# New positions for every task of a planned kernel (linear attention followed by a softplus layer)

## The chip, the cores and the metric

The kernel runs on one core of one Trainium2 chip. The metric is the device time of one execution in microseconds (us). TensorE is called PE, its weight loads PEld, VectorE DVE, ScalarE ACT, GpSimd POOL, and SyncE, which issues nearly all DMAs, SP.

## The reference

There are 8 batches of 8 heads, 576 tokens each, 64 wide. The second layer takes all 4608 tokens with 512 features.

```
kv  = einsum('bhsd,bhse->bhde', k, v)
out = einsum('bhsd,bhde->bhse', q, kv)
rms = sqrt(mean(out * out, axis=-1, keepdims=True) + 1e-06)
x   = (out / rms * g_norm)            # heads joined: 4608 x 512, float32
h   = x @ w_in                        # w_in 512 x 2048, float64
g   = maximum(h, 0) + log1p(exp(-abs(h)))
y   = g @ w_out                       # w_out 2048 x 512, float64; y float32
```

## The kernel before

All work is cut into some 3,000 tasks: a run of matmuls, one operation of ACT, DVE or POOL, or one DMA (or a few). Each task has an engine, a list of tasks that it follows, buffers ("slots" of numbered rings) that it takes and gives back, and a position, a number that says how urgent it is: less is earlier. A planner (`Plan.order`) runs the tasks through a model of the engines with fixed costs; whenever several tasks of an engine could start at about the same time, the one of the least position goes first. What comes out is an order for each engine, and the program is issued in it. The hardware then runs each engine's list strictly in that order and waits by semaphores. So positions change no instruction, only the order of each engine's list, and with it which buffer of a ring a task gets.

The stages overlap and are these:

- Attention, for each batch: k and v are loaded (`kv_of`, L706 and L704) and multiplied by five groups of products on PE (L717), the last of them for the tail of 64 tokens; ACT copies the result (L725). For each tile of 128 tokens (`rows`), q is loaded (L787; L620 for batches 2 to 7) and turned (on PE, L797, with a copy L804, or on DVE, L772), the row products (L741) follow, ACT squares (L814), DVE sums (L745), POOL takes the root (L748, L749), DVE multiplies (L753), and the result is turned again (L759 on PE with a copy, or L841 on DVE) and stored as x.
- Weights: w_in and w_out come as float64 words in 16 chunks of 128 (L434). ACT and DVE make float32 of them (`weight`: ACT L445 and L462, DVE L449, L453, L458, L466, L471, and L479 or L477), and split each into three rounded parts for fast products (`split_weight`, ACT L517 and L533, DVE L520 and L525). Chunks from the fifth on are also stored and loaded again later (`w_spill`).
- Plain steps: the first two blocks of 384 tokens are multiplied with chunks 0 to 3 in plain float32 (`plain_step`: first layer L934, softplus L954, second layer L940). Block 0 does its first two steps tile by tile.
- Chunk steps: the other ten blocks are multiplied with chunks 0 to 3 (blocks 2 and 3) or 0 to 5 in three rounded products each (`step`: L889 with twelve products, softplus L911, split L913, L900 and L904, second layer L896 with nine).
- Wide steps: for the other chunks, nine blocks of 512 tokens and two chunks at a time, by seven products instead of eight (`wide_step`, `units_of`). In each of 48 steps PE makes seven groups of six products (L1127, units 0 to 6) into one pair of banks. ACT copies partial results between banks (L1169 after units 0 and 1, L1173 after unit 3; unit 4 adds to what L1173 reads and copies), softplus follows (L1155), and the split (ACT L1185, DVE L1188 and L1191), then eight groups of three second-layer products (L1198). The steps form two phases; a block's sums are stored at the end of a phase and added at the start of the next (L970), and results leave by L991.
- While PE has nothing else to do at the start, the planner fills in warm-up products (L1292).

Where positions come from: constants of the lists P0 to P8 are added to a step number. P0 gives conversions and loads of the first weights (`CONVERT`, `FETCH`) and offsets of attention (`EARLY`), P1 the loads and splits of the wide stage's weight pairs 2 to 7 (`SPLIT`, first the load, then the split), P2 the loads and conversions of chunks 6 to 15 (`TAKEN`), P3 offsets within wide steps (`MM2`, `LATE`, `SPLIT_G`), P4 the tiles, P5 the batches, P6 the units of each wide block, P7 the loads of the first two batches, P8 the splits of the first four chunks (`DIVIDE`). One task sets the manner for all:

```python
small = [o for o in options if engine == "PE" and o[1].kind != "all"]
...
at, t = min(options, key=lambda o: (o[1].pos, o[0]))
```

and the wait that ties a DMA to a point of PE's progress, besides its buffer:

```python
for t in plan.tasks:
    if t.behind is not None and t.behind >= 0:
        t.after.append([m for at, m in mm1s if at <= t.behind][-1])
```

Of the kernel before, what the change touches and what calls it, by code (L numbers as in the profile page):

```python
# [60 lines left out]
class Plan:  # L61
# [19 lines left out]
    def slot(self, ring):  # L81
        return Slot(ring)

    def add(self, engine, ns, run, after=(), pos=0.0, take=(), give=(), size=0, behind=None, follows=None, kind="all"):
        pos, behind = round(pos, 4), None if behind is None else round(behind, 4)
        t = Task(engine, ns, run, [a for a in after if a is not None], pos, list(take), list(give), size)
        for s in t.give:
            s.readers += 1
        self.tasks.append(t)
        t.follows = follows  # L90
        t.behind = behind
        t.kind = kind
        return t
# [113 lines left out]
def kernel(  # L207
# [44 lines left out]
    STEPS = [(ph, n, p) for ph in (1, 2) for n in range(n_wide) for p in PAIRS[ph - 1][n]]  # L252
    LAST = 2

    P0 = [-31.3, -30.64, -54.26, -2.58, -36.38, -151.12, -27.16, 4.44, -244.63, -199.65, -214.44, -165.6, -164.44, -156.26, -159.89, -75.56, -23.5, -59.34, 26.17, 9.55, 6.93, 9.91, -11.55, 6.49, 1.74, 171.93, 45.23, 8.24, -1.35, 6.07]
    P4 = [-65.4, -44.7, 24.9, -3.29, -25.77, -68.08, -27.61, -41.6, -20.58, -7.41, -5.23, 2.97, 0.94, -0.53, -8.96, -41.17, 23.47, 21.42, -2.21, 21.68, 32.94, 28.75, -0.37, -0.34, 15.51, 20.06, -16.32, -5.39, 6.85, 4.85, -5.3, -4.14, 5.1, -2.49, -15.14, -6.44]
    P5 = [-6.87, 19.59, -28.05, -5.0, -6.56, -14.19, 6.28, -0.65, -1.35, 132.48, 5.39, 2.29, -35.85, 1.03, -3.98, -2.82]
    P6 = [1.5, 9.94, 2.49, -38.82, -78.8, -70.82, -46.98, -61.55, -42.52, -70.31, 9.49, -78.96, -19.23, -24.63, 6.03, 1.34, -86.15, 2.77]
    P7 = [-204.42, -204.37, -115.29, -133.71, -205.37, -112.22, -110.08, -112.78, -124.83, -118.61, -140.44, -143.0, -146.99, -143.39, -131.27, -137.05, -122.31, -132.54, -123.82, -86.56, -103.79, -107.89, -154.07, 73.6, -145.36, -62.81, -36.39, -58.6, 23.67, -42.55]
    CONVERT, FETCH, EARLY, LATER = P0[:8], P0[8:16], P0[16:27], P0[27:]  # L260
    P1 = [57.49, 48.45, 65.67, 68.82, 125.79, 131.21, 6.34, 52.11, 67.59, 160.94, 164.07, 162.57]
    P2 = [23.98, 35.63, 26.02, 37.56, 45.23, 74.16, 67.95, 125.34, 102.58, 112.94, 164.02, -30.15, 114.21, 131.81, 139.56, -30.3, 132.2, -22.69, 106.41, 131.82, -7.6]
    P3 = [1.03, 0.05, 7.95, -2.68, 0.96, 2.95, 4.31, -8.29, 3.44, 4.08, 0.91, 1.99, -0.13, -36.22, 0.66, -1.76]
    SPLIT = {p: (P1[i], P1[6 + i]) for i, p in enumerate((2, 3, 4, 5, 6, 7))}
    TAKEN = {c: (P2[c - 6], P2[4 + c]) for c in range(6, 16)}
    LEAD, APART, AHEAD, MM2, LATE, SPLIT_G = P3[0], P3[1], P3[2], P3[3:11], P3[11:14], P3[14]
    EARLIER = P3[15]
    P8 = [-29.7, 133.87, -29.82, -14.38, -36.33, 52.16, -9.84, -27.11]
    DIVIDE, BANKED, STORE, AFTER = P8, False, 1.0, 1.5
    BY_TILES, CHAIN = 2, False  # L270
    PACE = 2.5
# [338 lines left out]
    def load_q(b):  # L610


        q_slots[b], q_loads[b] = slot("qa"), []
        pos = x_pos(first_tile[b] + 1) - EARLY[7] + P5[B + b]

# [67 lines left out]
    def x_pos(t):  # L683

        n = t // TB
        return P4[t] + t * EARLY[0] + EARLY[1] if n == 0 else P4[t] + first_step["block", n] - (EARLY[2] if n == 1 else EARLY[3]) + t % TB * (len(CHUNKS[n]) // TB)

    def kv_of(b):

        pos = x_pos(first_tile[b]) - (EARLY[4] if b else EARLY[5]) + P5[b]
        bank = slot(f"s{b}" if b < 2 else "tp")
        last = first = None
        MAIN = 4 * P
        for p in range(NP + 1):
# [4 lines left out]
            def load(src, s, p=p, tail=tail, n=n, ks=ks):  # L701
                if tail:
                    s.tile = tails[s is not ks]
                    nc.sync.dma_start(out=s.tile[:n], in_=src[b, :, MAIN:].rearrange("h s d -> s h d"))  # L704
                    return
                nc.sync.dma_start(out=new(s, [P, 2, 4, D]), in_=src[b, p::NP, :MAIN].rearrange("h (s i) d -> s h i d", i=4))  # L706

            lds = [add("SP", 500, lambda src=src, s=s, load=load: load(src, s), (), pos - EARLY[6] + 0.5 * p + (P7[2 * (5 * b + p) + of_v] if b < 2 else 0), [s], [],
                       650 if tail else 850, behind=pos - 5.5) for of_v, (src, s) in enumerate(((k, ks), (v, vs)))]
# [18 lines left out]
    def rows(t):  # L728
# [38 lines left out]
        for b, r0, n, s0 in parts(t):  # L767
# [26 lines left out]
            def turn_q(n=n, q_s=q_s, at_qa=at_qa, tp=slot("tp" if t < AT_ONCE else "o")):  # L794
                y = new(tp, [P, NP, P])
                for p in range(NP):
                    nc.tensor.transpose(y[:, p, :n], pairs(natural(q_s, at_qa)[:n], p), ident[:n, :n])  # L797

            tp = turn_q.__defaults__[-1]
            ld = add("SP", 900, load, (), pos - EARLY[7] + P7[20 + t], [q_s] if not at_qa or t == 0 else [], [], 1220 * n // P,  # L800
                     behind=pos - 3.5, follows=first_load[0] if t and at_qa else None)
# [218 lines left out]
    def units_of(ph, n):  # L1020

        at = starts[first_of[ph, n]] - LEAD + P6[n_wide * (ph - 1) + n]
        held = {}
# [236 lines left out]
    for c in range(KF):  # L1260
        for j in (2 * c, 2 * c + 1):
# [3 lines left out]
            else:  # L1265
                fetch, pos = (x + P2[20] * (j % 2) for x in TAKEN[c])
                weight(j, pos, fetch, fetch)
# [60 lines left out]
```

## Time and profile before

| | |
|---|---|
| time, median of 3 runs | 863.43 us (863.42 to 865.5) |
| profiled execution | 863.93 us, its span 861.8 us, granted clock 0.999 |
| PE busy / PEld busy | 849.1 us (99%) / 742.5 us (86%) |
| DVE / ACT / POOL busy | 694.4 us (81%) / 489.5 us (57%) / 76.5 us (9%) |
| chain that ended last | PE 93%, DMA 4%, ACT 1%, DVE 1% |
| DMA | 167.06 MB, mean 194 GB/s |

The span runs from the first to the last instruction of the profiled execution; its time is 2.13 us longer. Ends of matmuls are modelled, so a short wait of PE shows as a longer distance between the starts of two products and not always as idle time. L1127 stands for line 1127 of the kernel; a line of the profile gives output and inputs by buffer names without their numbers, and `pieces`, `w`, `units`, `early` and others are pieces of memory that serve several rings.

### The profile page before, as it was taken

How to read it: one execution, taken by the hardware profiler on the slowest of the kernel's cores; microseconds unless marked ns; L12 is line 12 of the kernel's file. 1: busy time of each engine (PE TensorE's matmuls, PEld its weight loads, DVE VectorE, ACT ScalarE, POOL GpSimd, SP SyncE). 2: the span in 40 equal slices, each digit the busy share in tenths (PEclk: the TensorE clock that was granted, in tenths of full speed). 3: DMA queues.
4: the chain of work that ended last, by engine and by line, in shares of the span. 5: the costliest groups of instructions: out<-in, count | busy, mean ns of one | idle time of the engine just before them, and what ended most of it. 6: DMA issues, size and time to landing. Idle time of an engine off the chain costs nothing.

```text
span 861.8 us, 16844 instructions
## 1 busy us (share of the span) xinstructions
PE 849.1 (99%) x6405; PEld 742.5 (86%) x6405; DVE 694.4 (81%) x974; ACT 489.5 (57%) x921; POOL 76.5 (9%) x79
## 2 busy tenths in 40 slices
PE   7999999999999999999999999999999999999998
PEld 5755888999898999989988888889888989899986
DVE  4988898888788888898987788787878767778873
ACT  3656554445444556656656555555757555566654
POOL 0433142221113100000000000000000000000000
PEclk9999999999999999999999999999999999999999
DMA  9998999778882766447544545556445654677754
GB/s 260 269 246 272 250 233 277 160 241 229 220 187 80 198 189 197 135 134 233 184 143 143 179 139 192 172 158 215 144 158 167 204 167 138 216 223 242 245 179 138
DMA packets 239777, 167.06 MB, mean 194 GB/s; under 512 B 106320, under 2 KB 198736, under 8 KB 239696
## 3 DMA queue, kind: packets, MB, share of 16 engines
q1 hardware_dynamic: 239392, 165.86, 65.4%
q8 instruction: 50, 0.82, 0.4%
q14 instruction: 31, 0.25, 0.1%
q10 hardware_dynamic: 304, 0.13, 0.1%
HBM read 112.98 MB, written 52.95 MB: 193 GB/s over the span
## 4 chain that ended last, share of the span: by engine, by line
PE 93%; DMA 4%; ACT 1%; DVE 1%; SPq 1%; POOL 0%; issue 0%; ACTq 0%; DVEq 0%
PE banks L1198 30%; PE banks L1127 28%; PE banks L889 14%; PE banks L896 14%; PE banks L741 2%; PE banks L717 2%; PE banks L934 2%; PE banks L940 2%; DMA g<-in_moe_w_out_dram 1%; DMA m<-w_spill 1%; DMA raw<-in_moe_w_in_dram 1%; DMA loads<-in_v_dram 1%; DMA part<-m 1%; PE banks L759 0%; POOL roots L749 0%
## 5 line engine op out<-in xcount | busy, mean ns | idle before, releaser
L1198 PE MATMUL banks<-w,gv 128*128 128x512 f32 x408 | 126.4, 391 | 0.0
L1198 PE MATMUL banks<-pieces,gv 128*128 128x512 f32 x360 | 111.7, 391 | 0.0
L1127 PEld LDWEIGHTS banks<-units,w 128*128 128x128 f32 x744 | 97.5, 188 | 9.2 <-ACT banks L1173 5.2
L1127 PE MATMUL banks<-units,w 128*128 128x256 f32 x744 | 104.6, 284 | 0.1
L1188 DVE TENSOR_TENSOR gv<-gv,g_True 128x1024 fp32r<-128x1024 f32 x47 | 57.5, 1223 | 46.1 <-ACT gv L1185 46.1
L889 PE MATMUL banks<-units,pieces 128*128 128x384 f32 x480 | 91.3, 338 | 0.0
L889 PEld LDWEIGHTS banks<-units,pieces 128*128 128x128 f32 x480 | 84.2, 188 | 3.3 <-issue 0.5
L1127 PE MATMUL banks<-units,pieces 128*128 128x256 f32 x600 | 82.9, 282 | 0.0
L1127 PEld LDWEIGHTS banks<-units,pieces 128*128 128x128 f32 x600 | 78.6, 188 | 4.3 <-ACT banks L1173 0.7
L911 ACT ACTIVATE half<-banks 128x384 f32<-128x384 f32 x56 | 27.5, 490 | 92.9 <-PE banks L889 86.7
L1198 PE MATMUL banks<-w,g_False 128*128 128x512 f32 x204 | 79.3, 389 | 0.0
L1198 PEld LDWEIGHTS banks<-w,gv 128*128 128x128 f32 x408 | 70.5, 188 | 9.4
L1198 PE MATMUL banks<-pieces,g_False 128*128 128x512 f32 x180 | 70.1, 390 | 0.0
L1198 PEld LDWEIGHTS banks<-pieces,gv 128*128 128x128 f32 x360 | 61.5, 188 | 7.5
L896 PE MATMUL banks<-pieces,gv 128*128 128x512 f32 x270 | 67.0, 392 | 0.0
L749 POOL TENSOR_TENSOR roots<-roots,half 128x8 f32<-128x8 f32 x36 | 62.8, 1744 | 3.0
L1155 ACT ACTIVATE g_True<-banks 128x256 f32<-128x256 f32 x96 | 36.7, 384 | 45.8 <-PE banks L1127 44.9
L1090 DVE TENSOR_TENSOR units<-units,loads 128x1024 fp32r<-128x1024 f32 x42 | 51.3, 1221 | 11.3 <-ACT units L1087 10.9
L896 PE MATMUL banks<-w,gv 128*128 128x512 f32 x234 | 58.8, 393 | 0.2 <-DVE gv L904 0.2
L1191 DVE SCALAR_TENSOR_TENSOR g_False<-gv 128x1024 fp32r<-128x1024 f32 x47 | 57.5, 1223 | 1.1
L896 PEld LDWEIGHTS banks<-pieces,gv 128*128 128x128 f32 x270 | 50.0, 188 | 8.7
L1093 DVE SCALAR_TENSOR_TENSOR units<-units 128x1024 fp32r<-128x1024 f32 x42 | 51.4, 1224 | 2.3
(126 smaller groups left out, 1562.4 us busy)
## 6 DMA issues: line engine op xcount, KB each, us to landing
loads<-x SPq DMA_DIRECT2D x180, 128.0 KB, 2.6
part<-m SPq DMA_DIRECT2D x72, 256.0 KB, 3.1
m<-part SPq DMA_DIRECT2D x72, 256.0 KB, 3.8
loads<-form SPq DMA_DIRECT2D x45, 256.0 KB, 3.4
form<-loads SPq DMA_DIRECT2D x36, 256.0 KB, 2.5
raw<-in_moe_w_in_dram SPq DMA_DIRECT2D x16, 512.0 KB, 4.7
loads<-in_k_dram SPq DMA_DIRECT2D x30, 256.0 KB, 5.0
loads<-in_v_dram SPq DMA_DIRECT2D x30, 256.0 KB, 5.1
```

Of the source, the lines that this page charges most:

```text
L717: nc.tensor.matmul(kv[e * D:(e + 1) * D, i if tail else p], lhsT=l, rhs=r, start=(p == 0 and i == 0), stop=tail, skip_group_check=True)
L749: nc.gpsimd.tensor_tensor(out=r.tile, in0=r.tile, in1=half, op=ALU.pow)
L889: nc.tensor.matmul(from_the_end(hp, w), lhsT=w_in.tile[:, i, kd * P:(kd + 1) * P], rhs=from_the_end(xv.tile[:, i, kd], w), start=(m == 0), ...
L896: nc.tensor.matmul(mine[i].tile, lhsT=gv.tile[:, m, i * P:(i + 1) * P], rhs=w_out.tile[:, m], start=(c == cs[0] and m == 0), stop=(c == cs ...
L911: a = add("ACT", 490, lambda: nc.scalar.activation(new(g, [P, NT]), h.tile, func=AF.Softplus, scale=BACK), [a], s, [g], [h])
L1090: nc.vector.tensor_tensor(out=part_of(1, F32R), in0=part_of(0), in1=xl.tile if m > 1 else xl.tile[:, 0], op=ALU.subtract)
L1093: nc.vector.scalar_tensor_tensor(out=part_of(2, F32R), in0=part_of(1), scalar=RADIX, in1=part_of(0), op0=ALU.mult, op1=ALU.add)
L1127: nc.tensor.matmul(from_the_end(place(q), (16, 8)[kd]), lhsT=w[:, m, at:at + P], rhs=from_the_end(dst.tile[:, m, v, kd] if u < 6 else dst. ...
L1155: nc.scalar.activation(dst, src, func=AF.Softplus, scale=BACK)
L1188: nc.vector.tensor_tensor(out=gvt(1, F32R), in0=gvt(0), in1=gt(), op=ALU.subtract)
L1191: nc.vector.scalar_tensor_tensor(out=gt(F32R), in0=gvt(1), scalar=RADIX, in1=gvt(0), op0=ALU.mult, op1=ALU.add)
L1198: nc.tensor.matmul(from_the_end(mine[i].tile, P), lhsT=(gvt(m, F32R) if m < 2 else gt(F32R))[:, c, i * P:(i + 1) * P], rhs=from_the_end(ou ...
```

## The change

All numbers of P0, P1, P2, P3, P4, P5, P6, P7 and P8 are replaced. Nothing else is touched: the same tasks with the same dependencies, rings and model of the planner, and the first two blocks still in plain float32. The lists of all engines come out in a new order; the program has one warm-up product more (34 instead of 33) and otherwise the same instructions.

```diff
-    P0 = [-31.3, -30.64, -54.26, -2.58, -36.38, -151.12, -27.16, 4.44, -244.63, -199.65, -214.44, -165.6, -164.44, -156.26, -159.89, -75.56, -23.5, -59.34, 26.17, 9.55, 6.93, 9.91, -11.55, 6.49, 1.74, 171.93, 45.23, 8.24, -1.35, 6.07]
...
-    P7 = [-204.42, -204.37, -115.29, -133.71, -205.37, -112.22, -110.08, -112.78, -124.83, -118.61, -140.44, -143.0, -146.99, -143.39, -131.27, -137.05, -122.31, -132.54, -123.82, -86.56, -103.79, -107.89, -154.07, 73.6, -145.36, -62.81, -36.39, -58.6, 23.67, -42.55]
+    P0 = [-26.53, -8.6, -26.43, -24.39, -7.46, -30.31, -30.51, -0.46, -18.19, -11.95, -60.72, -23.11, -7.51, -6.45, -6.97, 1.51, -96.36, -87.58, 23.05, 9.66, 5.63, 70.22, -11.32, 5.48, 1.28, 13.64, -24.06, 10.03, 2.31, 2.8]
...
+    P7 = [223.82, 237.85, 234.17, 234.67, 233.72, 224.13, 258.05, 213.66, 244.82, 245.6, 18.63, 20.59, 18.78, -10.12, 26.9, 20.69, 26.52, 26.35, 25.8, 26.37, 159.02, 240.48, 142.45, 87.4, 36.17, 16.65, 55.56, 45.85, 25.93, -10.94]
     CONVERT, FETCH, EARLY, LATER = P0[:8], P0[8:16], P0[16:27], P0[27:]
-    P1 = [57.49, 48.45, 65.67, 68.82, 125.79, 131.21, 6.34, 52.11, 67.59, 160.94, 164.07, 162.57]
-    P2 = [23.98, 35.63, 26.02, 37.56, 45.23, 74.16, 67.95, 125.34, 102.58, 112.94, 164.02, -30.15, 114.21, 131.81, 139.56, -30.3, 132.2, -22.69, 106.41, 131.82, -7.6]
-    P3 = [1.03, 0.05, 7.95, -2.68, 0.96, 2.95, 4.31, -8.29, 3.44, 4.08, 0.91, 1.99, -0.13, -36.22, 0.66, -1.76]
+    P1 = [56.7, 48.36, 57.86, 71.7, 122.92, 131.34, 49.33, 64.2, 68.62, 81.9, 167.23, 29.07]
+    P2 = [26.08, 34.69, 22.87, 44.8, 34.85, 56.63, 53.72, 108.5, 124.7, 118.83, 132.01, -7.51, 132.17, 132.06, 131.34, -7.51, 127.41, 52.53, 132.4, 132.35, -6.49]
+    P3 = [0.23, 0.22, 10.44, -2.21, 0.7, 2.68, 4.22, -2.49, 2.69, 2.73, 0.68, 2.26, -0.04, -94.1, -87.17, -2.98]
     SPLIT = {p: (P1[i], P1[6 + i]) for i, p in enumerate((2, 3, 4, 5, 6, 7))}
     TAKEN = {c: (P2[c - 6], P2[4 + c]) for c in range(6, 16)}
     LEAD, APART, AHEAD, MM2, LATE, SPLIT_G = P3[0], P3[1], P3[2], P3[3:11], P3[11:14], P3[14]
     EARLIER = P3[15]
-    P8 = [-29.7, 133.87, -29.82, -14.38, -36.33, 52.16, -9.84, -27.11]
+    P8 = [-24.8, 69.82, -7.38, -23.22, -18.55, -21.72, -19.14, -30.61]
```

## The prediction

> **What bounds the kernel now.** I read the page's busy times first, then the busy times cut into stages, then TensorE's (PE's) timeline with what ended each gap, then the waits, and last the issue order of the two programs, which gives orders and no times.
>
> ```profile
> PE 849.1 (99%) x6405; PEld 742.5 (86%) x6405; DVE 694.4 (81%) x974; ACT 489.5 (57%) x921; POOL 76.5 (9%) x79
> ```
>
> ```profile
> 0.00:30.00 30.00, 23.41 (x306) 16.88 (x307) 17.76 (x33) 13.53 (x26) 4.95 (x11) 1.00 0.95 267
> 30.00:91.00 61.00, 59.72 (x615) 38.07 (x613) 53.10 (x88) 39.12 (x79) 21.62 (x20) 1.00 0.93 259
> 91.00:140.00 49.00, 48.22 (x594) 41.33 (x596) 43.27 (x75) 26.61 (x51) 15.03 (x15) 1.00 0.94 238
> 140.00:358.00 218.00, 217.88 (x1770) 197.64 (x1761) 184.27 (x315) 110.97 (x220) 34.94 (x34) 1.00 0.69 190
> 358.00:640.00 282.00, 282.00 (x1782) 253.19 (x1781) 235.83 (x288) 170.71 (x322) 0.00 (x0) 1.00 0.53 168
> 640.00:858.00 218.00, 217.83 (x1362) 195.34 (x1361) 159.67 (x177) 128.03 (x226) 0.00 (x0) 1.00 0.62 194
> ```
>
> The columns of the second table are the stretch in us, its length, busy us of PE, of PE's weight loads, of DVE, ACT and POOL, then the granted clock, the DMA share and GB/s. PE idles 6.6 us before 30 us, then 1.28, 0.78, 0.12, 0 and 0.17 us: 2.35 us in 828. DMA is over 0.9 busy until 140 us. So PE's own work bounds all that follows the start, and a new order can win only the start, these 2.35 us, and waits too short to show as idle. A sum over rows sizes the last: from 91.5 to 858 us stand 1152 products of L1198 and 504 of L896 at 0.227 us (2.04 for nine), 2016 of L1127 at 0.117 (2.10 for eighteen), 672 of L889 at 0.174 (2.09 for twelve), 729 us together; the attention products there take some 28 us (23 groups of L717 at 0.5, 25 of L741 at 0.65). That leaves about 9 us in 766 for all changes of shape and all waits; some 20 stretches of attention products at a quarter of a microsecond each are 5 of them, and 4 are waits.
>
> ```profile
> 19.49 0.69 PE L717 MATMUL banks<-m,m 128*64 128x64 f32 x16 [0.46 <-DMA m<-in_k_dram]
> 29.95 1.06 PE L934 MATMUL banks<-w,w 128*128 128x128 f32 x8
> 54.54 2.85 PE L934 MATMUL banks<-w,w 128*128 128x384 f32 x8
> 63.98 1.15 PE L717 MATMUL banks<-loads 128*64 128x64 f32 x32
> 117.68 0.69 PE L741 MATMUL banks<-early,w 64*64 64x64 f32 x32 [0.61 <-ACT half L911]
> ```
>
> ```profile
> 48.78 0.43 DVE L449 TENSOR_SCALAR m<-g 128x512 uint32<-128x512 uint32 x1 [0.83 <-DMA g<-in_moe_w_out_dram]
> 52.56 0.74 DVE L479 SCALAR_TENSOR_TENSOR w<-m,g_col,m 128x512 f32<-128x512 f32 x1
> ```
>
> These are the places where the start is decided: the last k load of batch 0 (19.49), the first plain product (29.95), the plain product of chunk 3 (54.54), which waited for a conversion (L479) queued behind that of another load (48.78), and the late k and v of batch 2 (63.98).
>
> ```profile
> 455.35 0.36 ACT L1173 COPY banks<-banks 128x256 f32<-128x256 f32 x1 [0.29 <-PE banks L1127]
> 455.76 1.50 PEld L1127 LDWEIGHTS banks<-units,w 128*128 128x128 f32 x12 [0.19 <-ACT banks L1173]
> 455.83 1.63 PE L1127 MATMUL banks<-units,w 128*128 128x256 f32 x12
> 457.30 0.63 PE L1198 MATMUL banks<-pieces,gv 128*128 128x512 f32 x2
> ```
>
> ```profile
> PEld banks L1127 <- ACT banks L1173: 5.9, 25, 0.6
> ```
>
> In the wide stage the weight loads waited 25 times for the copy L1173; here twelve products took 457.30 - 455.83 = 1.47 us instead of 1.40.
>
> **The change part by part.** No instruction is added or removed but one warm-up product (L1292, 33 to 34), which fills time that PE waits anyway: nothing. Every other cost is in the order.
>
> *Start.* In the issue order the last k load of batch 0 stays 16th in SP's queue, but 4352 KB stand up to it instead of 4224 (one v of batch 1 more, half a q tile less). At 267 GB/s the 128 KB are 0.5 us. What follows it to the first plain product (kv copy, two row products, two squares, two reduces, the pair of POOL roots at 2.0 us each, norm, transposition, copy) stands in the same order on ACT, DVE and POOL, with the weights of chunks 0 and 1 exchanged. So 29.95 becomes 30.4 (bounds 29.6 to 31, as the loads of w_in now go out third and not eighth).
>
> *To chunk 3.* Its w_in is now load 43 with 11920 KB up to it; before, load 43 with 12032 KB was the one that landed at 48.75. It lands at 48.3. The six conversions (0.42, 0.69, 0.69, 0.42, 0.75, 0.75) have one reduce (0.68) among them instead of a norm and the whole other conversion: ready at 52.8. PE has three groups fewer ahead of it (L759 0.44, L797 0.44, L741 0.47: 1.35), so PE on the old timing is due at 54.54 - 1.35 = 53.2. Whatever the start loses up to 0.4 us is absorbed here: net 0 (bounds -0.4 and +1.5, if the queue lags by two more k/v loads).
>
> *Late k and v of batch 2.* PE has five groups fewer ahead (0.44 + 0.86 + 2.58 + 0.44 + 0.47 = 4.8 us): due at 59.2. The last load was issued at 54.42 and is now 400 KB, 1.6 us, earlier: 52.9, plus the 6.3 us median to landing of that stretch (longest 7.1): 59.2 to 60.0. SP's queue behind it holds q loads of batch 2, which have slack. +0.2 (0 to 1.2).
>
> *Changes of shape.* Stretches of PE that leave the large products for kv or row products rise from 34 to 37, while direct kv-to-row changes fall from 7 to 4. Two kv groups in a row take 1.08 us, one alone 0.61: 0.14 for a visit on leaving, about 0.1 on entering. +0.3 (0 to 0.7).
>
> *91 to 140 us.* The row product that waited 0.61 us at 117.68 needs the bank of the one two tiles earlier; 4.9 us of PE work lay between them, now 6.9: gone (-0.6). The first L896 of the last chunk of block 2 comes 2.8 us of PE work after its L889 instead of 3.2, against ACT and DVE rows of 0.49 + 0.52 + 0.56 + 0.56 = 2.1 and some 0.5 of hand-overs: 0 to +0.5, I take 0.3. Net -0.3.
>
> *Wide stage, the copy L1173.* In 27 of the 48 steps of before exactly one product group (0.70 us) stands between the group whose result L1173 copies and the next group that writes there; now in 4. The place above is one of them: +0.07. The 23 others save 23 x 0.07 = 1.6 us; from below it is bounded by 0 (a copy behind a 1.06 us L1185 would wait all the same), from above by 23 x 0.11 = 2.5 (one LDWEIGHTS of L1127 late by more than a slot). I take -1.6. By the Trainium skill ("TensorE: Matmul & The Clock Gate", under "Architectural detail") PE pulls weight loads ahead of running products, and by that alone the wait would cost nothing and the sum would be 1.6 us higher; the trace disagrees, with 0.19 us of wait on the load and 1.47 for 1.40 on the products.
>
> *Wide stage, new tight places.* From the last group of a step to its first second-layer product before never had less than 4.8 us of PE work (bar the last step); now one step late in phase 2 has 4.2. The chain is 0.39 + 1.06 + 1.22 + 1.22 and 0.3 of hand-overs, 4.2, or 4.8 with a 0.63 softplus ahead: +0.3 (0 to 0.6). The split of the weights of pair 7 moves ahead of all other DVE and ACT work around 640 us (its position falls from 162.57 to 29.07), where DVE is 82% busy (81.97 of the 100 us from 600): +0.3 (0 to 1).
>
> Sum: 0 + 0.2 + 0.3 - 0.3 - 1.6 + 0.6 = -0.8. The span of 861.8 becomes 861.0; the profiled execution lies 2.13 us above its span (863.93), and 0.5 above the median 863.43, so the median comes to 862.6. 0.3% is 2.6 us, about what a measurement of this kernel can tell from no change.
>
> **The rivals.** *Slower: chunk 3's weight.* If the conversion of its w_in takes the 10 us that it took before (43.3 to 53.3) because its ACT half or the landing slips, it is ready at 58.3, 5.1 us after PE is due: 862.6 + 5.1 = 867.7. It decides past 8 us of conversion. For it: DMA at 0.93 and DVE at 87% of that stretch leave no reserve. Against: the order shows one foreign operation in it. 0.17.
>
> *Faster by more.* The other waits shrink too: half of the 2.35 us of idle and half of the 4 us of short waits, 3.2 us: 859.4. For it: the distances grew in most steps. Against: the tight places above. 0.22. The Trainium skill ("Perfetto Trace Analysis", Identifying the Most-Contended Engine) judges headroom by the share of LDWEIGHTS, not of matmuls; at 86% that would be up to 119 us to win. The rows speak against it: a product of 512 columns takes 0.227 us and its load 0.188, so the loader idles in a full pipe, and I give it no more than 0.02 of the 0.22.
>
> *The copy's wait only moves.* If L1173 now mostly queues behind ACT's longer rows (L1185 and L1087 at 1.06 us, L991 at 0.6), the 1.6 us stay: 864.2. For it: the order puts such a row ahead of it in many steps. Against: two groups of cover, 1.4 us, hold the copy's 0.36 and one of those rows but the longest. 0.2, still within 0.3%.
>
> **How the numbers follow.** The forecast has 0.41, the moved wait 0.2, the slower rival 0.17, the faster one 0.22. Faster by over 0.3% (under 860.8) takes the faster rival and a little of the forecast's low end: 0.24. Slower (over 866.0) takes the slower rival and a little of the unknown of the DMA order: 0.18. Within: 0.58. The range of 859.0 to 867.2 leaves out less than 2 in 10; the forecast's own is 860.8 to 864.6.
>
> **What would show it.** After: the first L934 near 30.4; the L934 x8 of chunk 3 near 53 with DVE L479 done just before; L717 of batch 2 with a short DMA wait near 59; L1173 gone from the top of the weight loader's waits (under 10 times), and no idle over 0.2 us on PE after 140. A w_in or w_out wait of several us on PE, DVE or ACT between 40 and 60 us, or DMA waits of L889 later, would make the forecast wrong.

## The result, and the profile after

The changed kernel takes 862.26 us (median of 22 runs, 860.01 to 863.9) against 863.6 us (22 runs, 861.94 to 866.08): 0.9982 of the time before, 95% interval 0.9974 to 0.9991. That is 1.3 to 1.6 us less, inside the 0.3% that was called no change, and 0.3 us from the forecast. The sum came out, by luck: its terms did not. Its profiled execution took 863.76 us with a span of 861.9.

The busy times of the page, then the same stages as before (length, busy us of PE, weight loads, DVE, ACT, POOL, then granted clock, DMA share, GB/s):

```profile
PE 848.6 (98%) x6406; PEld 746.0 (87%) x6406; DVE 695.5 (81%) x974; ACT 487.0 (57%) x921; POOL 78.6 (9%) x79
```

```profile
0.00:30.00 30.00, 23.20 (x261) 18.21 (x265) 16.06 (x30) 12.15 (x23) 4.94 (x11) 0.85 0.91 244
30.00:91.00 61.00, 59.20 (x660) 38.28 (x653) 53.25 (x89) 38.11 (x77) 24.98 (x20) 0.99 0.95 259
91.00:140.00 49.00, 48.87 (x543) 41.24 (x542) 42.85 (x72) 27.49 (x54) 9.57 (x10) 1.00 0.92 231
```

Nothing of the start is better: the clock is 0.85 in the first 30 us, where it was 1.00 (both views read 1.00 ahead of the trace's first entry for the clock, though the warm-ups stand 0.43 us apart there, and 0.23 from about 7 us on in the changed kernel, from about 11 before), and 30 to 91 us has 1.80 us of idle PE instead of 1.28. From 91 to 140 us the idle time fell from 0.78 to 0.13, as forecast. PE's timeline at the places where the start is decided:

```profile
11.47 1.97 PE L717 MATMUL banks<-loads 128*64 128x64 f32 x32 [2.85 <-DMA loads<-in_v_dram]
26.70 1.15 PE L717 MATMUL banks<-loads 128*64 128x64 f32 x32 [1.83 <-DMA loads<-in_v_dram]
32.65 1.95 PE L934 MATMUL banks<-w,w 128*128 128x128 f32 x16
55.50 2.84 PE L934 MATMUL banks<-w,w 128*128 128x384 f32 x8
62.36 1.15 PE L717 MATMUL banks<-loads 128*64 128x64 f32 x32
```

The first plain product starts at 32.65, not 30.4, chunk 3's at 55.50, not 53, and k and v of batch 2 (62.36) wait for no load. The L797 behind 26.70 takes 1.11 us where it took 0.66, at half clock. Late in the wide stage there is a wait that the forecast ruled out (no idle time over 0.2 us on PE after 140 us), lines of ACT, DVE and PE:

```profile
772.34 1.06 ACT L1087 ACTIVATE units<-loads 128x1024 fp32r<-128x1024 f32 x1 [2.40 <-DMA loads<-form]
774.58 0.68 DVE L1177 TENSOR_TENSOR g_True<-banks,g_True 128x512 f32<-128x512 f32 x1
775.32 0.98 PE L1127 MATMUL banks<-turned,half 128*128 128x256 f32 x6 [0.79 <-DVE g_True L1177]
```

A form loaded late holds ACT, DVE's L1090 queues behind ACT, and the L1177 that unit 6 needs queues behind that. What won the time shows as an absence. The row of the weight loader's waits that the prediction showed (5.9 us, 25 times) is now:

```profile
PEld banks L1127 <- ACT banks L1173: 0.4, 2, 0.2
```

To see where the time went, I took from each trace the distance from the start of one group of products to the start of the next, and subtracted what the same group takes undisturbed (L1127 0.70, a second-layer group L1198 0.68, and so on; changes of shape at their usual price). What is left is lost time, also where PE never shows as idle. Warm-ups count as lost. In the table "again" is a second profiled execution of the changed kernel.

| lost, us | before | after | again |
|---|---|---|---|
| up to the first L934 | 18.5 | 21.2 | 19.4 |
| to the first chunk step L889 | 2.8 | 3.6 | 3.6 |
| to the first L1127 | 4.4 | 3.4 | 3.6 |
| to the end | 7.1 | 4.3 | 3.8 |

The work ahead of the first L889 comes to the same 68.0 us in both kernels by this reckoning (the changed one has a group of L759 more there, two products of L940 fewer, and more changes of shape), so its start can be compared directly: 90.93 before, 94.43 and 92.68 after. The kernel loses 1.7 to 3.5 us at the start and wins 3.4 to 3.7 behind it.

### The profile page after: what moved, and what is told of

The parts are those of the page before. It is cut to its first block, busy times and chain, and to the rows that moved or that the text cites. A ratio compares the mean times of both kernels' runs of the same rounds, so it can differ in the third digit from the quotient of the medians.

```text
span 861.9 us, 16832 instructions
## 1 busy us (share of the span) xinstructions
PE 848.6 (98%) x6406; PEld 746.0 (87%) x6406; DVE 695.5 (81%) x974; ACT 487.0 (57%) x921; POOL 78.6 (9%) x79
## 4 chain that ended last, share of the span: by engine, by line
PE 92%; DMA 3%; DVE 2%; POOL 1%; ACT 1%; SPq 0%; issue 0%; ACTq 0%; DVEq 0%
PE banks L1198 29%; PE banks L1127 27%; PE banks L889 14%; PE banks L896 14%; PE banks L741 2%; PE banks L940 2%; PE banks L717 2%; PE banks L934 2%; DMA loads<-in_v_dram 1%; POOL roots L749 1%; DMA raw<-in_moe_w_in_dram 1%; PE banks L759 1%; DMA m<-in_k_dram 1%; DMA loads<-form 0%; DMA m<-part 0%
## 5 line engine op out<-in xcount | busy, mean ns | idle before, releaser
L1198 PE MATMUL banks<-w,gv 128*128 128x512 f32 x408 | 126.3, 391 | 0.0
L1198 PE MATMUL banks<-pieces,gv 128*128 128x512 f32 x360 | 111.2, 390 | 0.0
L1127 PEld LDWEIGHTS banks<-units,w 128*128 128x128 f32 x720 | 94.9, 188 | 5.6 <-ACT g_True L1152 0.4
L1127 PE MATMUL banks<-units,w 128*128 128x256 f32 x720 | 99.2, 281 | 0.0
L889 PE MATMUL banks<-units,pieces 128*128 128x384 f32 x480 | 91.4, 338 | 0.0
L889 PEld LDWEIGHTS banks<-units,pieces 128*128 128x128 f32 x480 | 84.2, 188 | 3.9 <-issue 1.0
L1127 PE MATMUL banks<-units,pieces 128*128 128x256 f32 x600 | 82.4, 281 | 0.0
L1127 PEld LDWEIGHTS banks<-units,pieces 128*128 128x128 f32 x600 | 78.5, 188 | 3.6 <-ACT banks L1173 0.2
L1188 DVE TENSOR_TENSOR gv<-gv,g_True 128x1024 fp32r<-128x1024 f32 x47 | 57.5, 1223 | 29.6 <-ACT gv L1185 29.5
L1198 PEld LDWEIGHTS banks<-w,gv 128*128 128x128 f32 x408 | 71.2, 188 | 10.5 <-DVE banks L970 0.4
L1198 PE MATMUL banks<-w,g_False 128*128 128x512 f32 x204 | 79.3, 389 | 0.0
L1198 PE MATMUL banks<-pieces,g_False 128*128 128x512 f32 x180 | 70.1, 389 | 0.0
L1198 PEld LDWEIGHTS banks<-pieces,gv 128*128 128x128 f32 x360 | 61.2, 188 | 6.9
L749 POOL TENSOR_TENSOR roots<-roots,half 128x8 f32<-128x8 f32 x36 | 64.9, 1802 | 3.0
L1090 DVE TENSOR_TENSOR units<-units,loads 128x1024 fp32r<-128x1024 f32 x41 | 50.0, 1220 | 12.8 <-ACT units L1087 12.8
L1177 DVE TENSOR_TENSOR g_True<-banks,g_True 128x512 f32<-128x512 f32 x48 | 33.1, 689 | 26.0 <-PE banks L1127 24.4
```

What stands on the lines that cost most here:

```text
L749: nc.gpsimd.tensor_tensor(out=r.tile, in0=r.tile, in1=half, op=ALU.pow)
L889: nc.tensor.matmul(from_the_end(hp, w), lhsT=w_in.tile[:, i, kd * P:(kd + 1) * P], rhs=from_the_end(xv.tile[:, i, kd], w), start=(m == 0), ...
L1090: nc.vector.tensor_tensor(out=part_of(1, F32R), in0=part_of(0), in1=xl.tile if m > 1 else xl.tile[:, 0], op=ALU.subtract)
L1127: nc.tensor.matmul(from_the_end(place(q), (16, 8)[kd]), lhsT=w[:, m, at:at + P], rhs=from_the_end(dst.tile[:, m, v, kd] if u < 6 else dst. ...
L1177: d = add("DVE", 700, lambda: nc.vector.tensor_tensor(out=gt()[:, :, HW:], in0=ab.tile[:, 1].rearrange("r (q t) -> r q t", q=2), in1=gt()[ ...
L1188: nc.vector.tensor_tensor(out=gvt(1, F32R), in0=gvt(0), in1=gt(), op=ALU.subtract)
```

## Experiments

All run against the kernel before on the same chip. Times of different groups of runs differ by about a microsecond, so ratios are compared. Orders are edited after the planner has made them; buffers stay as planned.

**The changed kernel again**

> The changed kernel itself, as a yardstick beside the others. Both theories: 862.3 +- 0.6 against about 863.6 for the kernel before. Its profiled execution of above showed a granted clock of 0.50 from about 10.9 to 17.2 us and from 27.9 to 31 us, after two holes of PE (2.85 and 1.83 us). If the clock falls because of the holes, this execution shows it again in the same two places; if it fell by chance in that one execution, the clock is 1.00 here.

861.71 us, 0.9967 (0.9955 to 0.9979). The clock fell again after the first hole, here 3.44 us (0.73 over 10.9 to 17.2 us), but not at 27.9 to 31: the v load of batch 1 landed sooner, and the hole there was 0.63 us instead of 1.83. First L934 at 30.92, chunk 3 at 53.76, 22.84 us behind it as in the first execution (55.50 - 32.65 = 22.85). So the second fall belongs to the second hole, and the start of this kernel varies by 1.7 us from one execution to the other with the landing of its loads.

**Holes of PE filled with warm-up products**

```diff
+    for t in done:
+        if t is kv[5]:            # first group of batch 1
+            more(7)
         t.run()
+        if t is warm_ups[17]:
+            more(12)
```

> The changed kernel with 19 more warm-up products: 12 behind the 18 first ones (PE idles there from 8.6 to 11.5 us) and 7 ahead of the first kv group of batch 1 (24.9 to 26.7 us). Nothing else is moved. Theory 1 (PE's holes lower the granted clock, and the products at half clock delay the path of the start): clock 1.00 in 10 to 32 us, L797 there 0.66 and not 1.11, the x32 of L741 0.69 and not 1.13, the first L934 1.4 us earlier (31.2 against 32.65), and the time 1.0 to 1.4 us under that of the changed kernel. Theory 2 (loads alone set the start: the v load of batch 1 lands at 26.6): clock 1.00 too, but the first L934 stays after 32.2 and the time is the same within 0.4 us. Theory 3 (the gain is made at the start and lost at chunk 3, whose weight L479 was done 0.06 us ahead of its products at 55.5): first L934 earlier, L934 of chunk 3 still at 55.3 to 55.6.

861.97 us, 0.9971 (0.9958 to 0.9984): the same as the changed kernel. The stretch of the second fall, first in the changed kernel, then here:

```profile
27.90:31.00 3.10, 3.10 (x40) 2.54 (x41) 1.86 (x4) 1.36 (x3) 1.43 (x1) 0.50 1.05 296
```

```profile
27.90:31.00 3.10, 3.04 (x80) 2.28 (x76) 2.62 (x6) 1.83 (x4) 1.30 (x1) 1.00 1.07 320
```

The clock is 1.00 throughout, and 3.1 us hold 80 products instead of 40. From the kv group of batch 1 to the first L934 it takes 4.60 us (26.90 to 31.50); in the slow-clock execution it took 5.95 from nearly the same point (26.70). So the fall cost 1.35 us there. But the time is no lower: seven warm-ups hold that group until 26.90 even if its load is there at 25.5. And the profile is of one execution: of the eight runs here three show a mean clock of 0.998 or less, of the 22 of the changed kernel 19. Theory 1 is right on the clock and not borne out on the time, which is what theory 2 gave; theory 3 is refuted, since chunk 3 stands 22.85 behind the first L934 here too. By the Trainium skill ("TensorE: Matmul & The Clock Gate", Part 1) PE falls to half clock after an idle window of some 3.4 us and the window runs freely; the trace agrees on the half, and shows that holes of 2.85 and 1.83 us were enough in the changed kernel, while one of 1.79 us in this run (ahead of 20.39) was not, nor one of 3.11 us (ahead of 11.18) in the changed kernel's run with a later start, below. The length of a hole does not decide. In the changed kernel's first execution the clock changes at 7.29, 10.70, 17.53, 27.77 and 31.18 us, whole multiples of 3.41 apart, and so it does in every trace. The stretch of this length just ahead of the second fall, and the emptiest one at the start of the run with the later start (columns as above; the number behind the length is PE's busy time):

```profile
24.36:27.77 3.41, 1.53 (x36) 1.37 (x36) 3.34 (x7) 1.32 (x4) 2.45 (x4) 1.00 0.83 161
```

```profile
9.54:12.96 3.42, 1.78 (x39) 1.55 (x41) 2.53 (x5) 1.45 (x4) 0.00 (x0) 1.00 1.01 245
```

In all ten traces, cut into such stretches from the first entry for the clock on, it fell behind each one in which PE was busy for 1.53 us or less (1.33 and 1.53 in the first execution, 1.32 in the second) and behind none with 1.78 or more. The hole of 3.11 us is divided between two stretches, the one shown and one with 1.94.

**Unit 4 one group closer, in the changed kernel**

```diff
+    for u3, c6, u4 in triples:    # c6: the copy L1173
+        order = [t for t in done if t.engine == "PE"]
+        i, j = order.index(u3), order.index(u4)
+        if j - i > 2:
+            at = done.index(order[i + 2])
+            if done.index(c6) < at:
+                done.remove(u4)
+                done.insert(at, u4)
```

> The changed kernel, but in 35 of the 44 wide steps where two or more product groups stand between unit 3 and unit 4, unit 4 is moved up so that only one does. ACT's order is unchanged. Theory 1 (a copy L1173 with one group of 0.70 us behind it makes unit 4 wait 0.07 to 0.11 us, as it did in 27 steps of before): 35 x 0.08 = 2.8 us slower than the changed kernel (2.4 to 3.9), and about 35 waits of the weight loader for L1173. Theory 2 (the loader fetches weights ahead and hides it): same time, no more waits than 4.

869.88 us, 1.0066 (1.0051 to 1.0081): 8.2 us over the changed kernel, three times what theory 1 gave. The row of the weight loader's waits:

```profile
PEld banks L1127 <- ACT banks L1173: 8.6, 37, 0.4
```

The number of waits is as expected (37) and the unit 4 groups are long by 0.11 as expected. But 8.2 / 35 = 0.23 us are lost per place, not 0.08; by the distances between groups the 37 places lose 8.7 us in this trace, 0.23 each too.

**Unit 3 one group earlier, in the kernel before**

```diff
+    for c1, u3, u4 in triples:    # c1: the copy L1169 that unit 3 needs
+        order = [t for t in done if t.engine == "PE"]
+        i, j = order.index(u3), order.index(u4)
+        at = done.index(order[i - 1])
+        if j - i == 2 and done.index(c1) < at:
+            done.remove(u3)
+            done.insert(at, u3)
```

> The kernel before, but in 24 of its 27 wide steps with one product group between unit 3 and unit 4, unit 3 is moved up by one group, so that two stand there. All else as before. Theory 1: 24 x 0.08 = 2.0 us faster than the kernel before (1.6 to 2.6), waits of the weight loader for L1173 down from 25 to 3 or 4. Theory 2 (the wait only moves, to L1169 ahead of unit 3 or to DVE behind): same time within 0.4 us.

859.22 us, 0.9945 (0.9929 to 0.9961): 5.1 us under the median of before by an edit of 24 places, 0.2 us each, and the lowest time of all versions here. Its interval overlaps that of the changed kernel (0.9967) by little. The step that the prediction showed, from the start of unit 4, here:

```profile
454.90 1.56 PE L1127 MATMUL banks<-units,w 128*128 128x256 f32 x12
456.30 0.62 PE L1198 MATMUL banks<-pieces,gv 128*128 128x512 f32 x2
...
461.14 0.62 PE L1198 MATMUL banks<-pieces,gv 128*128 128x512 f32 x2
```

and in the kernel before, the same nine groups (unit 4 at 455.83 as shown in the prediction), which end where the last line begins:

```profile
460.10 0.87 PE L1127 MATMUL banks<-units,pieces 128*128 128x256 f32 x6
460.81 0.88 PE L1127 MATMUL banks<-early,pieces 128*128 128x256 f32 x6
461.53 0.88 PE L1127 MATMUL banks<-early,w 128*128 128x256 f32 x6
462.25 0.63 PE L1198 MATMUL banks<-pieces,gv 128*128 128x512 f32 x2
```

The first twelve products take 1.40 here and 1.47 there: the 0.07 that the prediction read. But all nine groups take 461.14 - 454.90 = 6.24 against 462.25 - 455.83 = 6.42. Units 2, 0 and 1, 4 us behind the wait, start 0.71 and 0.72 apart instead of 0.70, with no wait of their own. So the wait has a tail, and it is larger than the 0.07 itself. Over the whole wide stage 25 such places lose 5.8 us in the trace of before, of which the unit 4 groups themselves are 2.2; in this run two places are left, 0.6 us. With the wait the long groups behind it are gone too, and in the run above they came with it: the tail belongs to the late load.

**The tail by itself**

```diff
+    for u5, u6 in pairs_56:
+        order = [t for t in done if t.engine == "PE"]
+        i, j = order.index(u5), order.index(u6)
+        if j - i == 3 and all(t in seconds for t in order[i + 1:j] + order[j + 1:j + 2]):
+            old, new_at = done.index(u6), done.index(order[j + 1])
...
+                done.remove(u6)
+                done.insert(new_at, u6)
```

> The kernel before with all its 27 places where unit 4 waits for the copy L1173. In 9 of these steps two second-layer groups follow unit 5, then unit 6, then one more second-layer group; here unit 6 is moved behind that third one, nothing else. In the trace of before such a step runs unit 4 at 809 ns (699 undisturbed), then unit 5 at 720, two groups at 694 and 695 (680 undisturbed), unit 6 at 718, one at 693, units 2, 0 and 1 at 720 each and three groups at 694, 695 and 690 until all is as undisturbed again. Theory 1 (one late weight load takes the loader's lead; groups run long until three second-layer groups in a row, whose products are longer than their loads, give it back): unit 6 and units 2, 0 and 1 of these 9 steps run at 700, the sum of what such a step loses falls from about 0.26 to 0.17 us, and the time by 9 x 0.1 = 0.9 us at most. Theory 2 (the later groups wait for something of their own): they stay at 720, time the same. Unit 6 is 0.7 us later for the softplus behind it; if that chain had no room, the time goes up by up to 9 x 0.7.

863.26 us, 1.0002 (0.9990 to 1.0014): too small an edit for the time to tell. Unit 6 moves in ten steps, in eight of which unit 4 waits. The same step, units 2 and 1 and the group behind them, with three second-layer groups in a row ahead of unit 6:

```profile
460.31 0.86 PE L1127 MATMUL banks<-units,pieces 128*128 128x256 f32 x6
461.71 0.86 PE L1127 MATMUL banks<-early,w 128*128 128x256 f32 x6
462.41 0.62 PE L1198 MATMUL banks<-pieces,gv 128*128 128x512 f32 x2
```

All 0.70 apart, though unit 4 waited here as before: the nine groups take 462.41 - 456.07 = 6.34 instead of 6.42, and the places of L1173 lose 4.9 us in this trace instead of 5.8. But a second trace of the order of before does the same without the edit. It is that of the kernel before with a later start, the next experiment, whose wide stage has the order of before, group for group; there unit 6 still follows two second-layer groups:

```profile
460.25 0.86 PE L1127 MATMUL banks<-units,pieces 128*128 128x256 f32 x6
461.64 0.86 PE L1127 MATMUL banks<-early,w 128*128 128x256 f32 x6
462.35 0.62 PE L1198 MATMUL banks<-pieces,gv 128*128 128x512 f32 x2
```

Its nine groups take 462.35 - 456.00 = 6.35, in all eight steps it loses what the edited order loses, to 0.01 us, and its places of L1173 lose 4.9 us in all, too. So the shorter tail is not the work of the edit: the tail of one and the same order differs between two executions, 0.2 us a place in one and 0.23 in the other. That three second-layer groups end it (theory 1) is not shown. Theory 2 does not hold either: where the order is the same and the tail is not, the later groups have no wait of their own.

**A later start, in both kernels**

In both, warm-up products ahead of the first kv group of batch 1 (`more(12)` in the kernel before, `more(16)` in the changed one).

> The kernel before with 12 more warm-up products ahead of the first kv group of batch 1, which then starts 2.2 to 2.6 us later than its 24.2. Theory 1 (the weight of chunk 3 sets the end of the start; PE has slack before it): the first L934 moves from 29.95 to about 32, the L934 x8 of chunk 3 from 54.54 by 1 us or less, and the time rises by less than 1 us. Theory 2 (what the start loses is lost 1 for 1): chunk 3 at 56.6 and the time 2 us up.

> The changed kernel with 16 more warm-up products ahead of the first kv group of batch 1, which then starts at about 28.5 instead of 25.5 to 26.7. Theory 1 (in the changed kernel a loss of the start is passed on whole: in three executions chunk 3's L934 x8 stood 22.84 us behind the first L934, whether that was 30.92 or 32.65): first L934 at about 33, chunk 3 at 22.84 behind it, the time 1.5 to 2.5 us up. Theory 2 (chunk 3's weight sets the end, as in the kernel before): chunk 3 stays at 54 to 55.5 and the time is up by less than 0.7.

The kernel before: 863.17 us, 1.0002 (0.9991 to 1.0013). The changed kernel: 863.17 us, 0.9999 (0.9985 to 1.0012), which is 1.5 to 2.8 us more than its own two ratios give without the edit, as theory 1 has it. The kv group, the first L934 and chunk 3's product, the kernel before first:

```profile
25.91 1.15 PE L717 MATMUL banks<-loads 128*64 128x64 f32 x32
30.51 1.06 PE L934 MATMUL banks<-w,w 128*128 128x128 f32 x8
54.66 2.85 PE L934 MATMUL banks<-w,w 128*128 128x384 f32 x8
```

```profile
27.59 1.15 PE L717 MATMUL banks<-loads 128*64 128x64 f32 x32
32.20 1.95 PE L934 MATMUL banks<-w,w 128*128 128x128 f32 x16
55.04 2.84 PE L934 MATMUL banks<-w,w 128*128 128x384 f32 x8
```

Before, 1.7 us at the kv group become 0.56 at the first L934 and 0.12 at chunk 3: absorbed, and the time stays. In the changed kernel chunk 3 stands 22.84 behind the first L934, as in all its other traces: nothing is absorbed. Neither delay became as large as planned, since the loads came at other times; in the changed kernel the first L934 (32.20) even lies between those of the two executions without the edit (30.92 and 32.65), so this trace shows the constant distance, not the loss of the median.

**One edit more on the best order**

```diff
+    order = groups()
+    at = order.index(rows_done[16])
+    step = order[at + 1]          # L889, block 3, second chunk
...
+    ahead(step, rows_done[16])
```

> The kernel before with unit 3 moved up by one group in 24 steps (as in the run that took 859.22) and one more edit: the first-layer group of block 3's second chunk goes ahead of the row product of tile 16, which waited 0.61 us at 117.68. Theory 1 (the wait was for a bank that comes free 4.9 us of PE work later; 2.1 us of other work now stand ahead): no wait there, 0.6 to 0.7 us under that run, 858.5. Theory 2 (the wait moves to the next row product or to the chunk's softplus): 859.2 again.

859.89 us, 0.9962 (0.9947 to 0.9977): nothing won.

```profile
120.50 0.69 PE L741 MATMUL banks<-early,w 64*64 64x64 f32 x32 [1.51 <-ACT half L814]
```

Tile 16 waits no more, but it now runs at 118.29, and what stands behind it in the queues with it: a norm L753 on DVE waits 1.09 us for PE and starts at 119.12, a square L814 on ACT waits 0.97 us for that and starts at 119.85, and tile 17 waits 1.51 us for the square, to 120.50. Theory 2, and worse than it said.

## Why the prediction was right, and where it was not

The total is right by luck: the gain at the copy was 3 to 4 us larger than reckoned, and the start and the new tight places, reckoned at 0.8 together, cost 5.8 us in the first execution (3.5 and 2.3) and 3.5 in the second (1.7 and 1.8).

- **Wide stage, the copy L1173: right place, price too low by three.** The prediction took 23 x 0.07 = -1.6 with -2.5 as its end. The places lose 5.8 us in the trace of before, 4.9 in the second trace of its order, and 0.6 after: 0.19 to 0.22 each, and the two edits give 0.2 and 0.23 each on the clock of the whole run. The failed step is "here twelve products took 1.47 us instead of 1.40": it measured the wait over the two groups next to it and stopped. The tail of three to twelve more groups, 0.01 to 0.02 each, was in the same trace. So was the room for it: the prediction reckoned 4 us of short waits, and the distances between groups show 7.1 in the wide stage alone. The rule weighed there (PE pulls weight loads ahead, Trainium skill, "TensorE: Matmul & The Clock Gate", "Architectural detail") did not hide the wait, as said. Why a late load has a tail stays open. A guess that fits the rows is that the loader loses its lead: a load takes 0.188 us and a product of L1198 0.227, so the loader would gain there, and little in L1127, whose products come every 0.117. But no run shows it, and it does not say why two groups of L1198 ended the tail in one execution and not in the other.
- **Wide stage, new tight places: too low.** Predicted +0.6; the traces show 2.3 and 1.8 us lost at places that the kernel before did not have. About 1.0 to 1.3 of it is the late form at 769 to 775 us, which the trace with filled holes does not show at all; about 0.6 is at 825 us, half of it a unit 2 that waits for a copy (L1152) queued on ACT, half a second-layer group behind it that waits for DVE's L970. The prediction looked at the second-layer chain and at pair 7, and at none of these.
- **Start: direction right, size wrong.** Predicted 30.4 for the first L934, bounds 29.6 to 31; three executions show 32.65, 30.92 and 32.01, four of before's start 29.95, 29.39, 30.18 and 29.24. The last k load of batch 0 did come late by about the 0.5 that was reckoned (20.06 and 20.10 against 19.49). In nine of the ten traces the first L934 starts, to 0.01 us, 6.93 us behind the first reduce L745 or 4.60 us behind the kv group of batch 1, whichever comes later; the tenth is the first execution of the changed kernel, where the half clock added 1.35. Both came late. The reduce stands behind a conversion of w_in on DVE (L449, L453, L458), and that waits for its load; on DVE, before and then the second execution of the changed kernel:

```profile
21.08 0.43 DVE L449 TENSOR_SCALAR m<-raw 128x512 uint32<-128x512 uint32 x1 [0.57 <-DMA raw<-in_moe_w_in_dram]
23.01 1.28 DVE L745 TENSOR_REDUCE roots<-half 128x8 f32<-128x512 f32 x2
```

```profile
22.12 0.43 DVE L449 TENSOR_SCALAR m<-raw 128x512 uint32<-128x512 uint32 x1 [0.32 <-DMA raw<-in_moe_w_in_dram]
23.99 1.27 DVE L745 TENSOR_REDUCE roots<-half 128x8 f32<-128x512 f32 x2
```

L745 started at 24.30, 23.99 and 25.09 instead of 23.01, which gives 31.23, 30.92 and 32.02. The step that failed is "what follows it stands in the same order on ACT, DVE and POOL": the order is the same, but what stands in it ahead of the reduce was put at nothing, and the square was ready 0.4 to 0.7 us before DVE was done with the conversion. PE was left out too: the last load that the kv group needs was issued at 19.71 and not 18.60, behind four q loads and not two, and the group started at 25.5 to 26.7 instead of 23.5 to 24.8. That decided in the first execution alone, and by little (31.30 against 31.23), ahead of the 1.35.
- **"Whatever the start loses up to 0.4 us is absorbed": wrong for this order.** Chunk 3's weight was ready 0.06 us ahead of its product in every trace of the changed kernel; DVE works nearly without a gap from 36.9 us to that conversion (0.8 us idle of 18.5), and its queue begins with tile 2's L753, which hangs on the start (on the kv group in the first execution, on the reduces in the second). The slower rival, a conversion of 10 us, did not happen: it took 4.4 us (50.98 to 55.43) and only began late.
- **91 to 140 us and batch 2: right.** Idle time 0.78 to 0.13; no load waited for near 60 us. **Changes of shape:** +0.5 remains in the sums for them, +0.3 was predicted.
- **The faster rival** had the right mechanism (short waits shrink with the distances), the rest of its gain went at the start. **The moved wait** did not come: L1173 holds the loader 2 times instead of 25.

## What to carry to other kernels

On an engine that is never idle, price a wait by the distance over ten or more groups behind it, not by the stretched pair: here the tail was 1.3 to 1.6 times the loss of the group that waited. Compare an edited trace with more than one trace of the order without the edit: one tail was short in both. When loads or conversions are reordered, follow the order of every engine up to the point that the next stage needs, the matmul queue too, and ask whether that point has slack; the same lost microsecond was free in one order and paid in full in the other. Before rearranging everything, look for the one pair that is too close in most steps: moving one task in 24 places gave more (0.9945) than all new positions (0.9982 and 0.9967).

## What was not expected of the hardware

- A weight load that came late made its own group long by 0.05 to 0.11 us and the next 3 to 12 groups by 0.01 to 0.02 us each (0.72 for 0.70, 0.694 for 0.680). How many differed between two executions of the same order (5.8 and 4.9 us over its places).
- PE's granted clock fell to 0.50 after holes of 2.85 and 1.83 us, for 6.8 and 3.4 us, and did not after one of 3.11 us in another run. What went with the falls is PE's busy time in stretches of 3.41 us: 1.53 us or less ahead of each, 1.78 or more elsewhere. In the profiled execution with the holes filled with products of no use it stayed at 1.00.
